# A decode-step kernel on one core: the last 128-row tile of the output weights goes to 32 partitions in four small loads

## The chip, the cores and the metric

The kernel runs on one core of a Trainium2 chip. The metric is the device time of one execution in microseconds (us). Five engines work side by side: PE (TensorE, matrix products; it loads its stationary operand with a weight load, "PEld", ahead of each matmul), DVE (VectorE), ACT (ScalarE), POOL (GpSimd) and SP (SyncE, which here only issues transfers). They wait for each other on semaphores. Transfers between DRAM and the on-chip memory are carried by 16 DMA engines.

## The reference: what is computed

One token for each of 4 sequences, model width 512. From `x` (4 x 512) a layer norm gives `xn`, and the result is `x + s * g`, where

- `s` is an attention over the last W = 1024 rows of a cache: 32 query heads share 8 key/value heads of width 128, so that each key/value head `g` serves 4 query heads. `q = xn @ wq`, then softmax of `q k^T / sqrt(128)`, times `v`, and last the projection `o @ wo` with `wo` of 4096 x 512;
- `g = silu(gelu(layernorm(xn) @ w1 + b1) @ w2 + b2)`, with `w1` 512 x 1792 and `w2` 1792 x 512.

Everything is bf16 in DRAM. About 29 MB are read: 8 MB each for the used parts of the keys and values, 4 MB for `wq`, 3.5 MB for `w1` and `w2`, and 4 MB for `wo`.

## The kernel before, in words

The order of the work is written out by hand. `_Program` keeps one list of operations for each engine (`pe`, `dve`, `act`, `gp`, `sp`); an operation names the operations it depends on, and `emit` puts a semaphore wait ahead of it. Each engine runs its list in order, so the order of the lists is the schedule. A DMA has a semaphore of its own, which must reach 16.

**Transfers.** SP issues nearly all of them in one queue, in this order: half of `wq`, keys of heads 0 and 1, the other half of `wq`, keys 2 to 7, values 0, `w1`, values 1, `w2`, values 2 to 7, and then `wo` in six loads (lines 470 to 476), called here load 0 to load 5. Loads 0, 1 and 2 bring two heads each (1 MB, 4 KB in a row of the DMA), load 3 brings head 6 (512 KB), load 4 brings three quarters of head 7 (rows with `i` = 0 to 2, 384 KB, 3 KB in a row), and load 5 the last quarter (`i` = 3, 128 KB, 1 KB in a row). ACT issues the small ones: `x`, `b1`, `b2` and, at line 251, `x` once more as 16 rows of 128 (`x16`, two loads of 8 rows).

**Attention.** For each head, PE transposes the keys (`T`, line 278), DVE copies them out of PSUM (line 284), PE forms the scores (`S`, lines 293 and 297), ACT takes the exponential (line 305). Then for each head `PV` (line 315) multiplies by the values, a matmul by ones (line 321) forms the denominators, and `epilogue` on DVE (lines 328 to 333) divides and writes `OTb`.

**MLP.** `mlp1` to `mlp4` are put between the `PV`s of the first heads. `mlp1` multiplies by `w1` in rows: 16 matmuls of 512 columns and four for the bias (lines 400 to 408); it is the last reader of `w1_sb`. The result `g_sb` is ready at 58 us.

**Output projection.** `to_rows` (line 478) spreads the normalized outputs of all heads over the partitions: 16 small matmuls with a selection matrix `sel` that POOL builds at the start (line 231), and one DVE copy to `OW` (line 493). Then `wo(k, rows)` (line 499) runs for loads 0 to 5 in order: for each 128-row tile (head `g`, quarter `i`) four matmuls of 128 columns (line 507), 128 matmuls in all, all adding into one place in PSUM (`psM`). Each `wo(k)` waits for its load. So load 0 has 32 matmuls, loads 1 and 2 have 32 each, load 3 has 16, load 4 has 12 and load 5 has 4.

**Tail.** DVE multiplies by `g` (line 534), PE transposes (line 538), DVE adds `x16` (line 540), SP writes the 4 KB out (line 542) and waits for it.

Of the kernel before, what the change touches and what calls it, by code (L numbers as in the profile page):

```python
# [16 lines left out]
class _Program:  # L17
# [10 lines left out]
    def add(self, eng, fn, *deps):  # L28
        op = _Op(eng, fn, deps)
        self.ops[eng].append(op)  # L30
        return op
# [42 lines left out]
def bass_recurrent_scan__sliding_block_cached__mixer_channel_mlp__decode_kernel(  # L74
# [20 lines left out]
    B, D = 4, 512  # L95
# [26 lines left out]
    wo_sb = sb([128, HKV, 4, D], BF16)  # L122
    w1_sb = sb([128, 4, F], BF16)
    w2_sb = sb([128, FC, D], BF16)
    kt_buf = sb([128, NKT, UT * 128], BF16)
    P_buf = sb([128, HKV, NC * 16], BF16)

# [30 lines left out]
    b1_sb = sb([1, F], BF16)  # L158
    b2_sb = sb([4, 128], BF16)
    sel = sb([128, 4, 32], BF16)  # L160
    OW = sb([128, 4, HKV * 4], BF16)
    hT = sb([128, 64], BF16)

    OTb = sb([128, HKV * 16], BF16)
# [39 lines left out]
    def load_v(g):  # L204
        d_v[g] = pg.dma("sp", "v%d" % g, lambda e: e.dma_start(  # L205
            kv_buf[:, (HKV + g) % NS, :, :].rearrange("p c d -> p (c d)"), cache_rows(A_v_cache, g)),
            t_last[(HKV + g) % NS] if HKV + g >= NS else None)
# [11 lines left out]
    for g in range(2, HKV):  # L219
# [11 lines left out]
    c_sel = add("gp", lambda e: e.affine_select(  # L231
        sel[:, :, :], ones_bf[:, :], [[1, 4], [4, 32]], ALU.is_equal, 0.0,
        base=0, channel_multiplier=-1), c_1)
    c_xT = add("gp", lambda e: e.memset(xT[:, :, :], 0.0))
    c_yT = add("gp", lambda e: e.memset(yT[:, :, :], 0.0))
    c_z = add("gp", lambda e: e.memset(zero_bf[:, :], 0.0))
# [11 lines left out]
    v = add("dve", lambda e: e.bn_aggr(mv1[:, :], st1[:, :]), v)  # L248
    v = add("dve", lambda e: e.tensor_single_scalar(vt1[:, :], mv1[:, 1:2], EPS, ALU.add), v)
    a = add("act", lambda e: e.activation(sq1[:, :], vt1[:, :], AF.Sqrt), v)  # L250
    d_x16 = [pg.dma("act", "x16%d" % i, lambda e, i=i: e.dma_start(
        x16[8 * i:8 * i + 8, :], x_r[8 * i:8 * i + 8, :])) for i in range(2)]
    v = add("dve", lambda e: e.reciprocal(rstd1[:, :], sq1[:, :]), a)
    v = add("dve", lambda e: e.tensor_scalar(xn32[:, :], x32[:, :], mv1[:, 0:1], rstd1[:, 0:1],
                                             op0=ALU.subtract, op1=ALU.mult), v)
# [53 lines left out]
    def PV(g):  # L309
        pso = psO[g % 2]  # L310

        def fn(pe):
            last = None
            for c in range(NC):
                last = pe.matmul(pso[:, 0:16], kv_buf[:, (HKV + g) % NS, c, :],  # L315
                                 P_buf[:, g, c * 16:(c + 1) * 16],
                                 start=(c == 0), stop=(c == NC - 1))
            return last
        pv_op[g] = add("pe", fn, ex[g], d_v[g], ep[g - 2] if g >= 2 else None)

        den[g] = add("pe", lambda pe: pe.matmul(psS[g % 2][:, 0:512], ones_bf[:, :], P_buf[:, g, :],  # L321
                                                start=True, stop=True),
                     ex[HKV - 2 + g % 2], ep[g - 2] if g >= 2 else None)

    def epilogue(g):
        pso = psO[g % 2]
        cs = slice(g * 16, (g + 1) * 16)
        v = add("dve", lambda e: e.tensor_reduce(  # L328
            den_sb[:, cs], bass.AP(psS[g % 2], 0, [[512, 128], [1, 16], [16, NC]]),
            AX.X, ALU.add), den[g])  # L330
        v = add("dve", lambda e: e.reciprocal(rden[:, cs], den_sb[:, cs]), v)  # L331

        ep[g] = add("dve", lambda e: e.tensor_tensor(  # L333
            bass.AP(OTb, g * 16, [[HKV * 16, 128], [1, 4], [4, 4]]),
            pso[:, 0:16], rden[:, cs], ALU.mult), v, pv_op[g])
# [59 lines left out]
    def mlp1():  # L395
        def fn(pe):
            last = None
            for c in range(4):
                for s in range(4):
                    pe.matmul(psK[0][32 * s:32 * s + 32, 0:1024].bitcast(F32), yT[:, c, :],  # L400
                              bass.AP(w1_sb, c * F + K0[s], [[4 * F, 128], [1, 4], [FC, 128]]),
                              start=(c == 0), stop=False, tile_position=(0, 32 * s))
            for s in range(4):
                last = pe.matmul(psK[0][32 * s:32 * s + 32, 0:1024].bitcast(F32),
                                 ones_bf[0:1, 0:32],
                                 bass.AP(b1_sb, K0[s], [[F, 1], [1, 4], [FC, 128]]),
                                 start=False, stop=True, tile_position=(0, 32 * s))
            return last
        t = add("pe", fn, v_xyT, d_w1, d_b1, *[cp[n] for n in range(NUN - NB, NUN)])
        a = add("act", lambda e: e.activation(f32k(0), h_ps, AF.Square), t)  # L410
        v = add("dve", lambda e: e.scalar_tensor_tensor(f32k(1), f32k(0), 1.0 / GELU_K, h_ps,  # L411
                                                        op0=ALU.add, op1=ALU.mult), a)
        mlp["t"] = add("act", lambda e: e.activation(f32k(2), f32k(1), AF.Tanh,
                                                     scale=GELU_C * GELU_K), v)

    def mlp2():
        v = add("dve", lambda e: e.tensor_scalar(f32k(3), f32k(2), 0.5, 0.5,
                                                 op0=ALU.mult, op1=ALU.add), mlp["t"])
        v = add("dve", lambda e: e.tensor_tensor(hb, f32k(3), h_ps, ALU.mult), v)  # L419

        def fn(pe):
            last = None
            for t in range(4):
                last = pe.transpose(psK[2][:, t * 128:(t + 1) * 128],  # L424
                                    kt_buf[:, 4, t * 128:(t + 1) * 128], ident[:, :])
            return last
        t = add("pe", fn, v, cp[NUN - 1], cp[NUN - 2])

        mlp["h"] = add("dve", lambda e: e.tensor_copy(
            bass.AP(hT, 0, [[64, 128], [4, 16], [1, 4]]),  # L430
            bass.AP(psK[2], 0, [[1024, 128], [32, 16], [1, 4]])), t)

    def mlp3():
        def fn(pe):
            last = pe.matmul(psM[:, PS_Z:PS_Z + 16], b2_sb[:, :],
                             bass.AP(ident, 0, [[128, 4], [1, 4], [0, 4]]),
                             start=True, stop=False, skip_group_check=True)
            for k in range(FC):
                s = min(k // 4, 2) if k < FC - 4 else 3
                n = (k - K0[s]) * 16 + s * 4  # L440
                for c in range(4):
                    last = pe.matmul(psM[:, PS_Z + c * 4:PS_Z + (c + 1) * 4],
                                     w2_sb[:, k, c * 128:(c + 1) * 128], hT[:, n:n + 4],
                                     start=False, stop=(k == FC - 1), skip_group_check=True)
            return last
        t = add("pe", fn, mlp["h"], d_w2, d_b2, c_id)
        mlp["tz"] = add("act", lambda e: e.activation(
            tz_sb[:, :], psM[:, PS_Z:PS_Z + 16], AF.Tanh, scale=0.5), t)
# [17 lines left out]
        w2_sb[:, :, :], B_w2.rearrange("(p c) o -> p c o", c=FC)))  # L466
    for g in range(2, HKV):
        load_v(g)

    wo_r = A_wo.rearrange("(g p i) o -> p g i o", g=HKV, i=4)  # L470
    d_wo = []
    for n, (g0, g1, i0, i1) in enumerate(((0, 2, 0, 4), (2, 4, 0, 4), (4, 6, 0, 4), (6, 7, 0, 4),
                                          (7, 8, 0, 3), (7, 8, 3, 4))):
        d_wo.append((g0, g1, i0, i1, pg.dma("sp", "wo%d" % n, lambda e, g0=g0, g1=g1, i0=i0, i1=i1:
                                            e.dma_start(wo_sb[:, g0:g1, i0:i1, :],  # L475
                                                        wo_r[:, g0:g1, i0:i1, :]))))

    def to_rows(g0, g1):

        psx = psS[0]  # L480

        def fn(pe):
            last = None
            for i in range(4):
                for j in range(4):
                    last = pe.matmul(psx[32 * j:32 * j + 32, i * 32 + g0 * 4:i * 32 + g1 * 4],
                                     sel[:, i, :],
                                     bass.AP(OTb, g0 * 16 + j * 4,
                                             [[HKV * 16, 128], [16, g1 - g0], [1, 4]]),
                                     start=True, stop=True)  # L490
            return last
        t = add("pe", fn, ep[g1 - 1], c_sel, ex[HKV - 2])
        return add("dve", lambda e: e.tensor_copy(
            OW[:, :, g0 * 4:g1 * 4],
            psx[:, 0:128].rearrange("p (i n) -> p i n", i=4)[:, :, g0 * 4:g1 * 4]), t)

# [16 lines left out]
            return last  # L513
        return add("pe", fn, d, rows, mlp["g"])

    for g in range(HKV):
        PV(g)
        if g == 0:
            epilogue(0)
            mlp1()  # L520
        if g >= 2:
            epilogue(g - 1)
        if g == 1:
            mlp2()
            mlp3()
        if g == 2:
            mlp4()
    epilogue(HKV - 1)
    rows = to_rows(0, HKV)
    for k in range(len(d_wo)):  # L530
        t_w = wo(k, rows)


    v = add("dve", lambda e: e.tensor_tensor(  # L534
# [61 lines left out]
```

## Time and profile before

| what | value |
|---|---|
| time, median of 3 runs | 77.09 us (77.07 to 77.11) |
| profiled execution, its own time | 77.07 us |
| span of that execution in the profile | 75.3 us (1.8 us lie around it) |
| busy: PE, PEld, DVE, ACT, POOL | 50.0, 39.8, 39.3, 9.8, 4.6 us |
| DMA | 28.99 MB, mean 385 GB/s |
| 42 to 67 us | DMA share 1.00 to 1.01, 420 GB/s; granted PE clock 0.82, then 0.50 |
| 70.0 to 72.5 us | DMA share 0.40, PE busy 2.30 us, granted clock 0.50 |
| 72.5 to 75.3 us | the tail: 0.38 us of PE, 0.46 us of DVE |

The profile shows one execution. Times inside it are counted from the start of the span. The granted clock is the share of its full speed at which PE was allowed to run. Matmuls are pipelined: a matmul that is shown with 166 ns can start 27 ns after the one ahead of it. "issue" as the cause of an idle time means that the engine waited for nothing that the profile shows. A DMA that is spread over all 16 DMA engines counts its semaphore up 16 times, once as each engine's share lands, and the trace has the time of each of the sixteen. The trace also has every packet that a DMA engine moved (start, duration, size, queue), though not the engine's number.

### The profile page before, as it was taken

The numbers are of one execution on the slowest core, as the hardware profiler recorded it, in microseconds if no ns is written. First come the engines' busy times: TensorE is split into PE (matmuls) and PEld (weight loads), VectorE is DVE, ScalarE is ACT, GpSimd is POOL, SyncE is SP. The second block draws the span as 40 slices with busy tenths as digits, with TensorE's granted clock in tenths as the row PEclk, the third lists the DMA queues.
The fourth block names the chain that finished last, engine by engine and source line by source line (L and its number), as shares of the span: only waits on it lengthen the run. The fifth ranks groups of instructions, "written<-read, shape, count | busy, mean of one in ns | idle before, by whom it ended". The sixth has DMA issues, their size and how long they took to land.

```text
span 75.3 us, 2297 instructions
## 1 busy us (share of the span) xinstructions
PE 50.0 (66%) x1046; PEld 39.8 (53%) x1058; DVE 39.3 (52%) x82; ACT 9.8 (13%) x16; POOL 4.6 (6%) x14
## 2 busy tenths in 40 slices
PE   0000039993859949987997994999069879818770
PEld 0000039992359939976997860104049576518740
DVE  0778107786058967985996424001664679770010
ACT  0611000000090303111130630003300000000000
POOL 6980000000000000000000000000000000000000
PEclk9999999999999999999999999569755555555555
DMA  1899999998999999999999999999999999999600
GB/s 36 244 455 405 420 422 479 435 444 370 427 422 431 422 418 431 427 414 466 401 420 453 406 443 390 427 431 409 427 427 440 418 401 416 418 420 416 252 25 2
DMA packets 4219, 28.99 MB, mean 385 GB/s; under 512 B 493, under 2 KB 625, under 8 KB 1650
## 3 DMA queue, kind: packets, MB, share of 16 engines
q1 hardware_dynamic: 4160, 28.84, 92.2%
q8 instruction: 8, 0.13, 0.6%
q10 hardware_dynamic: 50, 0.01, 0.1%
q14 instruction: 1, 0.01, 0.0%
HBM read 28.85 MB, written 0.00 MB: 383 GB/s over the span
## 4 chain that ended last, share of the span: by engine, by line
DMA 36%; PE 35%; SPq 16%; issue 5%; DVE 4%
DMA wo_sb<-in_A_wo_dram 24%; PE psK L278 22%; SPq L475 15%; DMA kv_buf<-in_A_k_cache_dram 12%; PE psS L297 7%; PE psO L362 3%; DVE kt_buf L284 2%; DVE q_sb L368 1%; PE psK L374 1%; PE psM L507 1%; PE psK L346 1%; PE psS L538 1%; SPq L212 1%; SPq L205 0%; DVE o_bf L540 0%
## 5 line engine op out<-in xcount | busy, mean ns | idle before, releaser
L278 PE MATMUL psK<-ident,kv_buf 128*128 128x128 bf16 x256 | 21.2, 237 | 11.8 <-DMA kv_buf<-in_A_k_cache_dram 10.6
L284 DVE COPY kt_buf<-psK 128x1024 bf16<-128x1024 bf16 x32 | 21.3, 691 | 8.7 <-PE psK L278 8.6
L278 PEld LDWEIGHTS psK<-ident,kv_buf 128*128 128x128 bf16 x256 | 17.1, 108 | 11.1 <-DMA kv_buf<-in_A_k_cache_dram 10.6
L297 PE MATMUL psS<-qT,kt_buf 128*128 128x16 bf16 x256 | 10.4, 169 | 1.7 <-issue 1.1
L297 PEld LDWEIGHTS psS<-qT,kt_buf 128*128 128x128 bf16 x256 | 9.4, 96 | 3.0 <-issue 2.1
L315 PEld LDWEIGHTS psO<-P_buf,kv_buf 128*128 128x128 bf16 x256 | 7.4, 102 | 3.0 <-issue 3.0
L315 PE MATMUL psO<-P_buf,kv_buf 128*128 128x16 bf16 x256 | 8.0, 173 | 1.0 <-DVE OTb L333 0.6
L328 DVE TENSOR_REDUCE den_sb<-psS 128x16 f32<-128x512 f32 x8 | 5.5, 691 | 4.2 <-PE psO L315 4.0
L305 ACT ACTIVATE P_buf<-psS 128x512 bf16<-128x512 f32 x8 | 4.8, 597 | 17.1 <-PE psS L297 17.1
L400 PE MATMUL psK<-w_sb,yT 128*32 128x512 bf16 x16 | 4.9, 1093 | 1.3 <-issue 1.3
L507 PE MATMUL psM<-OW,wo_sb 128*128 128x4 bf16 x128 | 3.9, 166 | 1.1 <-issue 0.6
L507 PEld LDWEIGHTS psM<-OW,wo_sb 128*128 128x128 bf16 x128 | 3.6, 104 | 1.4 <-issue 1.2
L411 DVE SCALAR_TENSOR_TENSOR kt_buf<-kt_buf,psK 128x512 f32<-128x512 f32 x1 | 0.7, 686 | 6.4 <-ACT kt_buf L410 6.4
L534 DVE TENSOR_TENSOR sg_sb<-psM,g_sb 128x16 f32<-128x16 f32 x1 | 0.2, 185 | 4.7 <-PE psM L507 4.7
L400 PEld LDWEIGHTS psK<-w_sb,yT 128*32 128x32 bf16 x16 | 0.5, 114 | 3.8 <-issue 3.8
L369 ACT ACTIVATE q_sb<-psO 128x512 bf16<-128x512 f32 x1 | 0.6, 597 | 13.5 <-PE psO L362 13.5
L424 PE MATMUL psK<-ident,kt_buf 128*128 128x128 bf16 x4 | 0.6, 307 | 2.4 <-DVE kt_buf L419 2.4
L331 DVE RECIPROCAL rden<-den_sb 128x16 f32<-128x16 f32 x8 | 2.0, 253 | 0.3
L362 PE MATMUL psO<-wq_sb,xT 128*32 128x512 bf16 x32 | 1.9, 380 | 0.3 <-DVE xT L351 0.3
L246 DVE CAST P_buf<-x_bf 4x512 f32<-4x512 bf16 x1 | 0.8, 795 | 2.4 <-DMA x_bf<-in_A_x_dram 2.4
L237 POOL TENSOR_SCALAR_AFFINE_SELECT negm<-zero_bf 128x512 bf16<-128x512 bf16 x1 | 1.9, 1852 | 0.1
L321 PE MATMUL psS<-P_buf,ones_bf 128*128 128x512 bf16 x3 | 1.8, 587 | 0.0
(64 smaller groups left out, 27.4 us busy)
## 6 DMA issues: line engine op xcount, KB each, us to landing
kv_buf<-in_A_k_cache_dram SPq DMA_DIRECT2D x8, 1024.0 KB, 19.9
kv_buf<-in_A_v_cache_dram SPq DMA_DIRECT2D x8, 1024.0 KB, 22.8
wq_sb<-in_A_wq_dram SPq DMA_DIRECT2D x2, 2048.0 KB, 11.3
w_sb<-in_B_w_dram SPq DMA_DIRECT2D x2, 1792.0 KB, 27.9
wo_sb<-in_A_wo_dram SPq DMA_DIRECT2D x3, 1024.0 KB, 24.3
wo_sb<-in_A_wo_dram SPq DMA_DIRECT2D x1, 512.0 KB, 21.5
wo_sb<-in_A_wo_dram SPq DMA_DIRECT2D x1, 384.0 KB, 18.2
wo_sb<-in_A_wo_dram SPq DMA_DIRECT2D x1, 128.0 KB, 18.0
```

The costliest lines, as they stand in the source:

```text
L237: c_neg = add("gp", lambda e: e.affine_select(negm[:, :], zero_bf[:, :], [[0, 32], [1, 4], [0, 4]], ALU.is_equal, NEG, base=0, channel_mul ...
L278: last = pe.transpose(psK[n % NB][:, j * 128:(j + 1) * 128], kv_buf[:, g, u * UT + j, :], ident[:, :])
L284: cp[n] = add("dve", lambda e: e.tensor_copy(kt_buf[:, n % NKT, :], psK[n % NB][:, 0:1024]), t, sc.get(n - NKT))
L297: last = pe.matmul(psS[g % 2][:, c * 16:(c + 1) * 16], kt_buf[:, n % NKT, j * 128:(j + 1) * 128], qT[:, g * 16:(g + 1) * 16], start=False, ...
L305: ex[g] = add("act", lambda e: e.activation(P_buf[:, g, :], psS[g % 2][:, 0:512], AF.Exp, scale=SCALE), sc[n])
L315: last = pe.matmul(pso[:, 0:16], kv_buf[:, (HKV + g) % NS, c, :], P_buf[:, g, c * 16:(c + 1) * 16], start=(c == 0), stop=(c == NC - 1))
L328: v = add("dve", lambda e: e.tensor_reduce(den_sb[:, cs], bass.AP(psS[g % 2], 0, [[512, 128], [1, 16], [16, NC]]), AX.X, ALU.add), den[g])
L331: v = add("dve", lambda e: e.reciprocal(rden[:, cs], den_sb[:, cs]), v)
L362: last = pe.matmul(psO[m // 4][32 * s:32 * s + 32, 0:512], xT[:, c, :], wq_sb[:, c, m * 512:(m + 1) * 512], start=(c == 0), stop=(c == 3), ...
L400: pe.matmul(psK[0][32 * s:32 * s + 32, 0:1024].bitcast(F32), yT[:, c, :], bass.AP(w1_sb, c * F + K0[s], [[4 * F, 128], [1, 4], [FC, 128]]) ...
L475: e.dma_start(wo_sb[:, g0:g1, i0:i1, :], wo_r[:, g0:g1, i0:i1, :]))))
L507: last = pe.matmul(psM[:, PS_W + c * 4:PS_W + (c + 1) * 4], wo_sb[:, g, i, c * 128:(c + 1) * 128], OW[:, i, g * 4:(g + 1) * 4], start=firs ...
```

## The change

Load 5, the 128-row tile of head 7 with `i` = 3, is no longer one load to 128 partitions. It becomes four loads of 32 rows of 1 KB each to partitions 0 to 31 of `wox_sb`, which lies in the memory of `w1_sb` (so they wait for the matmuls of `mlp1`). The DRAM side of each has an outermost dimension of 4 and an inner one of 8. They stand in SP's queue after load 3 and ahead of the rest of head 7, which now comes as a new load 4 (`i` = 0 and 1, 256 KB) and a new load 5 (`i` = 2, 128 KB). The bytes are the same. On PE, four matmuls of 128 rows are replaced by sixteen of 32 rows (`wo_x`), run after load 3's, and one matmul more in `to_rows` forms their other operand, which DVE copies to `OWx` in a copy of its own ahead of the copy to `OW`. POOL makes one more small constant (`selx`). Besides, `x16` comes in three loads of 7, 6 and 3 rows.

```diff
+    wox_sb = w1_sb[0:32, :, :].rearrange("p c f -> p (c f)")[:, 0:4 * D].rearrange(
+        "p (j o) -> p j o", j=4)
+    c_selx = add("gp", lambda e: e.tensor_copy(
+        selx[:, :], bass.AP(sel, 96, [[128, 128], [1, 4], [4, 8]])), c_sel)
...
-    d_x16 = [pg.dma("act", "x16%d" % i, lambda e, i=i: e.dma_start(
-        x16[8 * i:8 * i + 8, :], x_r[8 * i:8 * i + 8, :])) for i in range(2)]
+    d_x16 = [pg.dma("act", "x16%d" % i, lambda e, i=i, n=n: e.dma_start(
+        x16[i:n, :], x_r[i:n, :])) for i, n in ((0, 7), (7, 13), (13, 16))]
...
-    for n, (g0, g1, i0, i1) in enumerate(((0, 2, 0, 4), (2, 4, 0, 4), (4, 6, 0, 4), (6, 7, 0, 4),
-                                          (7, 8, 0, 3), (7, 8, 3, 4))):
...
+    for n, g0 in enumerate((0, 2, 4)):
+        load_wo(n, g0, g0 + 2, 0, 4)
+    load_wo(3, 6, 7, 0, 4)
+
+    for j in range(4):
+        d_wox.append(pg.dma("sp", "wox%d" % j, lambda e, j=j: e.dma_start(
+            wox_sb[:, j, :],
+            bass.AP(A_wo.tensor, (7 * 512 + 128 * j + 3) * D, [[4 * D, 4], [16 * D, 8], [1, D]])), mlp["w1"]))
+    load_wo(4, 7, 8, 0, 2)
+    load_wo(5, 7, 8, 2, 3)
...
     def to_rows(g0, g1):
...
+            last = pe.matmul(psx[0:32, 128:144], selx[:, :],
+                             OTb[:, 7 * 16:8 * 16], start=True, stop=True)
             return last
+        t = add("pe", fn, ep[g1 - 1], c_sel, c_selx, ex[HKV - 2])
+        rows_x = add("dve", lambda e: e.tensor_copy(OWx[:, :], psx[0:32, 128:144]), t)
...
+    def wo_x():
+        def fn(pe):
+            last = None
+            for j in range(4):
+                for c in range(4):
+                    last = pe.matmul(psM[:, PS_W + c * 4:PS_W + (c + 1) * 4],
+                                     wox_sb[:, j, c * 128:(c + 1) * 128],
+                                     OWx[:, j * 4:(j + 1) * 4],
+                                     start=False, stop=False, skip_group_check=True)
+            return last
+        return add("pe", fn, rows_x, *d_wox)
...
+    rows_x, rows = to_rows(0, HKV)
     for k in range(len(d_wo)):
         t_w = wo(k, rows)
+        if k == 3:
+            wo_x()
```

More of the change, by code (lines that the diff above doesn't have):

```diff
@@ L160, in bass_recurrent_scan__sliding_block_cached__mixer_channel_mlp__decode_kernel @@
     sel = sb([128, 4, 32], BF16)
+    selx = sb([128, 32], BF16)
     OW = sb([128, 4, HKV * 4], BF16)
+    OWx = sb([32, 16], BF16)
     hT = sb([128, 64], BF16)
@@ L408, in fn @@
             return last
-        t = add("pe", fn, v_xyT, d_w1, d_b1, *[cp[n] for n in range(NUN - NB, NUN)])
+        t = mlp["w1"] = add("pe", fn, v_xyT, d_w1, d_b1, *[cp[n] for n in range(NUN - NB, NUN)])
         a = add("act", lambda e: e.activation(f32k(0), h_ps, AF.Square), t)
@@ L468, in bass_recurrent_scan__sliding_block_cached__mixer_channel_mlp__decode_kernel, with load_wo @@
         load_v(g)
+    for g in range(HKV):
+        PV(g)
+        if g == 0:
+            epilogue(0)
+            mlp1()
+        if g >= 2:
+            epilogue(g - 1)
+        if g == 1:
+            mlp2()
+            mlp3()
+        if g == 2:
+            mlp4()
+    epilogue(HKV - 1)
     wo_r = A_wo.rearrange("(g p i) o -> p g i o", g=HKV, i=4)
     d_wo = []
-    for n, (g0, g1, i0, i1) in enumerate(((0, 2, 0, 4), (2, 4, 0, 4), (4, 6, 0, 4), (6, 7, 0, 4),
-                                          (7, 8, 0, 3), (7, 8, 3, 4))):
-        d_wo.append((g0, g1, i0, i1, pg.dma("sp", "wo%d" % n, lambda e, g0=g0, g1=g1, i0=i0, i1=i1:
-                                            e.dma_start(wo_sb[:, g0:g1, i0:i1, :],
-                                                        wo_r[:, g0:g1, i0:i1, :]))))
+    d_wox = []
+    def load_wo(n, g0, g1, i0, i1):
+        d_wo.append((g0, g1, i0, i1, pg.dma("sp", "wo%d" % n, lambda e: e.dma_start(
+            wo_sb[:, g0:g1, i0:i1, :], wo_r[:, g0:g1, i0:i1, :]))))
+    for n, g0 in enumerate((0, 2, 4)):
[7 more added lines that the diff above has]
+    load_wo(5, 7, 8, 2, 3)
     def to_rows(g0, g1):
@@ L490, in fn @@
                                      start=True, stop=True)
-            return last
-        t = add("pe", fn, ep[g1 - 1], c_sel, ex[HKV - 2])
-        return add("dve", lambda e: e.tensor_copy(
+            last = pe.matmul(psx[0:32, 128:144], selx[:, :],
+                             OTb[:, 7 * 16:8 * 16], start=True, stop=True)
+            return last
+        t = add("pe", fn, ep[g1 - 1], c_sel, c_selx, ex[HKV - 2])
+        rows_x = add("dve", lambda e: e.tensor_copy(OWx[:, :], psx[0:32, 128:144]), t)
+        return rows_x, add("dve", lambda e: e.tensor_copy(
             OW[:, :, g0 * 4:g1 * 4],
@@ L514, in wo @@
         return add("pe", fn, d, rows, mlp["g"])
[L516 to L529, printed above, removed]
+    def wo_x():
[10 more added lines that the diff above has]
+    rows_x, rows = to_rows(0, HKV)
     for k in range(len(d_wo)):
         t_w = wo(k, rows)
+        if k == 3:
+            wo_x()
     v = add("dve", lambda e: e.tensor_tensor(
```

## The prediction, made before the changed kernel ran

> **What bounds the kernel now.** I read three views in this order: the chain that ended last, PE's timeline over the last microseconds, and the DMA section of the page together with the sixteen landings of each load. The chain first (start, us, what):
>
> ```profile
> 53.69 18.16 DMA wo_sb<-in_A_wo_dram
> 71.86 0.05 issue
> 71.90 0.60 PE psM L507 x16
> 72.50 0.02 issue
> 72.52 0.20 DVE sg_sb L534
> ```
>
> The end hangs on load 4 of `wo`, which lands at 71.86, then on 16 matmuls (12 of load 4, 4 of load 5), then on the tail of 2.8 us, which the change doesn't touch. A reader could stop here and call the kernel bound by loads. PE's timeline says more:
>
> ```profile
> 67.19 0.30 PE L486 MATMUL psS<-OTb,sel 128*32 128x32 bf16 x16 [1.30 <-DVE OTb L333]
> 68.00 1.55 PE L507 MATMUL psM<-OW,wo_sb 128*128 128x4 bf16 x53 [0.51 <-DVE OW L493]
> 70.13 2.35 PE L507 MATMUL psM<-OW,wo_sb 128*128 128x4 bf16 x75 [0.58 <-issue]
> ```
>
> 53 matmuls take 1.55 us, one is shown with 0.166, so they start (1.55 - 0.166) / 52 = 26.7 ns apart (granted clock 0.50). Then PE stands for 0.58 us in the middle of load 1, which had landed at 67.06: it waits for no data. The DMA section names the other traffic:
>
> ```profile
> q8 instruction: 8, 0.13, 0.6%
> q14 instruction: 1, 0.01, 0.0%
> ```
>
> These are PE's instructions, in packets of 16 KB. The packet records have one at 67.84, and PE resumes 2.29 us after it; earlier ones at 25.51, 32.21 and 38.29 are followed by the chain's "issue" pieces, which end at 27.95, 34.43 and 40.45, 2.2 to 2.4 us later. So the stop is PE waiting for its program. From 70.13 on, 74 x 0.0267 + 0.166 = 2.14 us of the 2.35 are matmuls, and only 0.21 is the wait for load 4. **Loads and PE are nearly tied at the end**: what the loads gain beyond 0.21 us, PE does not pass on, and PE's own added work counts.
>
> The landings (us) of the last loads show why loads are late:
>
> ```
> load 3: 69.15 69.16 69.19 69.20 69.30 69.39 69.43 69.49 | 70.11 70.57 70.72 70.72 70.74 70.77 70.82 70.93
> load 4: 70.08 70.14 70.14 70.18 70.28 70.34 70.39 70.42 | 71.05 71.49 71.62 71.63 71.68 71.71 71.72 71.86
> load 5: 70.42 70.47 70.48 70.51 70.62 70.64 70.73 70.73 | 71.37 71.82 71.96 71.96 72.01 72.05 72.05 72.17
> ```
>
> Eight DMA engines are early, seven are some 1.4 us late, one 0.7 us; I take each to have carried one of the seven q8 packets up to 67.84 (0.88 to 0.96 us long), or the 8 KB q14 packet at 41.24 (0.31 us). Engines that work without a pause start a packet when the last one ends, to within 4 ns, so the packets can be strung into sixteen chains. The loads of 4 rows at the start (`x_bf`, `b2`) and of 1 row (`b1`) each land 4 times and once, and their packets lie in four of the chains; I take these to be the engines that a load spread over four uses. Three of the four are early (last data of load 5 at 70.15, 70.20, 70.29), **the fourth is the one with the q14 packet** (71.06, landing 71.37).
>
> **The loads, step by step.** 1 KB packets of load 5 start 42.4 ns apart, 3 KB packets of load 4 117.6 ns; 2 KB lies on the line between, 80 ns (estimate). Each engine has 8 rows of a full load.
> - The twelve other engines: 8 x 117.6 + 8 x 42.4 ns become 8 x 80 + 8 x 42.4, 0.30 us less. Their last landing goes from 72.17 to 71.87.
> - The four: 32 rows of 1 KB more, 32 x 42.4 = 1.36 us, four semaphore writes of 6 ns and one more `x16` row (20 ns) on some, less 0.30: +1.08 us. The three early ones land at 70.47 to 70.62 + 1.08 = 71.55 to 71.70. The late one lands at 71.37 + 1.08 = **72.45**, after the 72.17 of before.
> - The four loads land on the late engine at about 71.5 (its load 4 began at 69.77; + 1.38 + 0.31 from data to landing).
> - If such a load were spread over 16 engines instead, the bytes of each engine stay, and the last landing is 72.17 and four semaphore writes.
>
> The Trainium skill, "DMA: Bandwidth & Descriptors", section "Why a DMA increments its semaphore by 16 and not by 1", says the number of engines is the largest divisor up to 16 of the outermost dimensions of both sides, and that they are the lowest-numbered: with 4 and 32 here, four.
>
> **PE, step by step.** The program up to `to_rows` is unchanged on PE, so I let the stop end at 70.13 again. The added matmul of `to_rows` takes one pair of instructions, so 52 instead of 53 matmuls are ahead of the stop. After it come 128 - 4 + 16 - 52 = 88. PE reaches `wo_x` at 70.13 + 60 x 0.0267 = 71.73, when its loads are in, new load 4 at 72.16 (landed by 71.6 on the twelve, 72.11 on the late one) and new load 5 at 72.37. Alone it would end at 70.13 + 87 x 0.0267 + 0.166 = 72.62 against 72.48: +0.13 us. Two terms are not in the trace:
> - A pair with 32 rows: between 7 ns (line 486, 32 columns: (0.30 - 0.19) / 15) and 26.7 ns (line 507, the same 128 columns). I take 26.7; the other end saves 16 x 19.7 ns = 0.31 us.
> - The four semaphores that `wo_x` waits for are two more wait instructions of 51 ns. One ahead of line 538 (72.21) ran while matmuls kept their spacing: between 0 and 0.10 us, I take 0.
>
> The skill's "TensorE: Matmul & The Clock Gate", section "LDWEIGHTS (loading the stationary operand)", puts the price on columns and not on rows, like my choice. Against my stop speaks "Runtime: NRT & Kernel Launch", "Instruction fetch mechanics": crossing a block is "mostly hidden". The row has 0.58 us unhidden; with none PE would reach load 5 by about 71.8, and the loads alone would decide.
>
> **Sum.** New load 5 lands last at 72.45 on the late engine. Before, load 4's landing at 71.86 gave starts at 71.90, 71.95, 71.97, 72.00; so the last of four starts 0.14 after the landing and ends 0.17 later: 72.76 against 72.48, +0.28 us. This hides both unknown PE terms (72.37 + 0.10 is still ahead of 72.49). On the profiled execution: 77.07 + 0.28 = **77.35 us**; the median shown, 77.09, is 0.02 above it.
>
> **Costed at nothing.** DVE's added copy to `OWx` (0.17 to 0.29 us by lines 351 and 493) stands ahead of the copy to `OW`; `wo(0)` and all PE work up to the stop move by it, and the stop of 0.58 us swallows it; without that cover it costs 0.2 us. The added `to_rows` matmul likewise. POOL's `selx` (0.2 to 0.5 us beside its neighbours) delays `xT`, whose first reader is at 18.34, while POOL is through at 5.5. ACT's third `x16` issue (0.28 to 0.44 us) ends near 5.5; its next work starts at 6.79, on DVE. SP's four added issues (0.4 to 0.6 us each, up to 5.4 when the queue is full, as for load 5) come behind load 3's at 53.65; the queue then holds some 80 rows for each engine, so load 5 is issued by about 64, before 69 when it is needed. `mlp1`, which the four wait for, is through by 51.6. DVE's third wait for `x16` passes while PE transposes.
>
> **Rivals.**
> - *PE alone is the bound*: the q14 packet falls on none of the four engines. Then the last landing is 71.87 and PE ends 0.13 us later, 77.20 us, up to 77.30 with the waits. For it: the trace doesn't say what assigns that packet. Against: the three runs agree to 0.04 us, as they would if packets always fell alike.
> - *The loads' gain shows* (the other side, faster): place, the stop at 69.55. If PE's instructions come so early that the stop is under about 0.1 us, PE reaches load 5 by 71.87, and if no late engine is among the four, the end is 71.87 + 0.31 = 72.18: -0.30, 76.77 us. Cheap 32-row pairs alone, without a late engine, give -0.18, 76.89. It decides from 0.3 us less PE time on. Against: nothing ahead of the stop changes on PE.
> - *A 16 KB packet falls on one of the four*: that engine lands 1.08 after the latest now, about 73.2, and `wo_x` waits too: +1.0, 78.1 us. Against: none of seven did.
> - *The four loads use 16 engines*: last landing 72.2, reached by PE at 72.37: +0.13 or less, 77.1 to 77.2.
>
> **Chances.** Late engine among the four, 77.35 (77.25 to 77.45): 0.46. PE alone: 0.22, split between the bound of "same" on either side (0.08 same, 0.14 slower; a difference of 0.2%, 0.15 us, is about what can be told from none). Gain shows: 0.18. Packet on one of the four: 0.06. Sixteen engines: 0.08, same. Faster 0.18, same 0.16, slower 0.66. The range runs from the gain to well above the forecast, 76.75 to 77.6, and leaves out the 78.1.
>
> **What would show it.** Right: the landings of each `wox` load count four and not sixteen; the last landing of new load 5 stands alone near 72.45, the others end near 71.87; 52 or 53 matmuls of line 542 ahead of a stop of about 0.4 to 0.6 us ending at 70.1; no wait between load 3's matmuls and `wo_x`. Wrong: the stop missing or ending elsewhere; the last landing on an engine that got nothing more; sixteen matmuls of `wo_x` in much less than 0.43 us.

## The result and the profile after

| | median | all runs | profiled execution, its span |
|---|---|---|---|
| before | 77.09 us | 77.07 to 77.11 (4) | 77.07, 75.3 us |
| after | 77.69 us | 77.62 to 77.91 (4) | 77.91, 76.2 us |

The ratio is 1.0083 [1.0062, 1.0103]: slower by 0.60 us. The forecast was 77.35 in a range of 76.75 to 77.6, so the sign is right and the size is outside the range. The profiled execution of after is the slowest of its four, so its tail shows some 0.2 us more than the median.

The chain that ended last, of the kernel after (start, us, what):

```profile
49.56 22.05 DMA wo_sb<-in_A_wo_dram
71.61 0.05 issue
71.65 0.59 PE psM L542 x16
72.24 0.13 issue
72.37 0.56 PE psM L556 x16
72.94 0.49 PE psM L542 x12
73.43 0.02 issue
73.45 0.20 DVE sg_sb L570
```

Before, the last load named here was load 4, issued at 53.69, and DVE's `sg_sb` began at 72.52. Now it is load 3, issued at 49.56, a load that the change did not touch. It lands last at 71.61 (before: 70.93), and PE's work follows it nearly without a pause. The later loads are close behind, though: the sixteen matmuls of `wo_x` start at 72.37, 0.13 us after the last small load lands (72.24), and the last four matmuls start at 73.15, 0.05 us after the last landing of load 5 (73.10), and end at 73.41. That is 0.31 us after the landing, as in the forecast's sum. So load 3, the small loads and load 5 are nearly tied, and the chain view names the first of them. PE's timeline of after:

```profile
65.85 0.30 PE L518 MATMUL psS<-OTb,sel 128*32 128x32 bf16 x16 [1.30 <-DVE OTb L340]
66.73 1.53 PE L542 MATMUL psM<-OW,wo_sb 128*128 128x4 bf16 x52 [0.58 <-DVE OW L528]
68.85 0.46 PE L542 MATMUL psM<-OW,wo_sb 128*128 128x4 bf16 x12 [0.59 <-issue]
70.02 1.02 PE L542 MATMUL psM<-OW,wo_sb 128*128 128x4 bf16 x32 [0.70 <-DMA wo_sb<-in_A_wo_dram]
71.65 0.59 PE L542 MATMUL psM<-OW,wo_sb 128*128 128x4 bf16 x16 [0.62 <-DMA wo_sb<-in_A_wo_dram]
72.37 0.56 PE L556 MATMUL psM<-OWx,w_sb 32*128 32x4 bf16 x16
72.87 0.55 PE L542 MATMUL psM<-OW,wo_sb 128*128 128x4 bf16 x12
```

52 matmuls, then the stop of 0.59 us, as forecast, but 1.28 us earlier (it ends at 68.85 and not at 70.13). PE has time to spare now: it waits 0.70 us for load 2 and 0.62 us for load 3. The bracket of the fifth line is what to look at: a wait for load 3 was in no step of the forecast. The amount of instruction traffic is that of before:

```profile
q8 instruction: 8, 0.13, 0.6%
q14 instruction: 1, 0.01, 0.0%
```

Its place in time is not. PE's eighth 16 KB packet, at 71.74 before, comes at 69.98 here and lasts 1.13 us, beside the last loads. That alone does not make loads late: in runs 2 and 3 below it comes at 70.39 and 70.24, and load 5 lands by 72.27 and 72.17, within 0.1 us of before; and the slowest run, to partitions 64-79 and 96-111, has it at 71.78.

The landings of after (us):

```
load 3: 69.22 ... 69.75 (eight) | ... 71.61            before: 69.15 ... 69.49 | ... 70.93
wox 0:  69.77 69.89 70.04 | 71.16       wox 1: 70.26 70.39 70.52 | 71.57
wox 2:  70.75 70.83 70.90 | 71.91       wox 3: 71.06 71.20 71.35 | 72.24
load 5: 70.63 70.71 70.94 70.94 71.04 | 71.90 ... 72.49 72.69 | 73.10
```

Each `wox` load lands four times, three engines early and one late, and the last landing of load 5 stands alone. That is the forecast's picture; but the forecast had it at 72.45, with 71.87 for the latest of the others. From one small load to the next the late engine takes 0.33 to 0.41 us and the early ones at most 0.50, which leaves no room for a packet of 1.13 us: the rival that put a 16 KB packet on one of the four, at 78.1 us, is not what happened.

**Where the time came from.** The activity of each microsecond, kernel before and then kernel after (window, length, busy time and instructions of PE, PEld, DVE, ACT, POOL, then PE clock, DMA share, GB/s):

```profile
69.00:70.00 1.00, 0.55 (x21) 0.49 (x19) 0.00 (x0) 0.00 (x0) 0.00 (x0) 0.50 0.97 386
70.00:71.00 1.00, 0.87 (x33) 0.87 (x33) 0.00 (x0) 0.00 (x0) 0.00 (x0) 0.50 0.65 252
71.00:72.00 1.00, 0.94 (x35) 0.86 (x33) 0.00 (x0) 0.00 (x0) 0.00 (x0) 0.50 0.35 124
```

```profile
69.00:70.00 1.00, 0.31 (x12) 0.23 (x9) 0.00 (x0) 0.00 (x0) 0.00 (x0) 0.50 1.14 413
70.00:71.00 1.00, 0.98 (x32) 0.93 (x32) 0.00 (x0) 0.00 (x0) 0.00 (x0) 0.50 0.73 222
71.00:72.00 1.00, 0.38 (x15) 0.35 (x14) 0.00 (x0) 0.00 (x0) 0.00 (x0) 0.50 0.59 200
```

Read the last two columns together. From 70 to 71, before has its engines busy 0.65 of the time and moves 252 GB/s, 388 for a full share. After is busier, 0.73, and moves less, 222 GB/s: 304 for a full share. The engines are not idle and not given more bytes; their packets last longer. The packet records give the sizes: outside this stretch a 4 KB packet takes 159 ns, 3 KB 121, 2 KB 84 and 1 KB 46, nearly always to the nanosecond. In after, from about 69.9 to 70.6, most 4 KB packets take 200 to 271 ns, and many of 1 KB 50 to 80. I add up what the packets of loads to 73.6 us took over these four figures, from 69.0 on, and call it **lost packet time** (in us of a DMA engine, summed over all 16): 3.76 us in after, 0.21 in before.

### The profile page after: what moved, and what is told of

The parts are those of the page before. It is cut to its first block, busy times and chain, and to the rows that moved or that the text cites. A ratio compares the mean times of both kernels' runs of the same rounds, so it can differ in the third digit from the quotient of the medians.

```text
span 76.2 us, 2333 instructions
## 1 busy us (share of the span) xinstructions
PE 49.9 (66%) x1059; PEld 39.4 (52%) x1071; DVE 39.6 (52%) x83; ACT 9.8 (13%) x16; POOL 4.8 (6%) x15
## 4 chain that ended last, share of the span: by engine, by line
DMA 41%; PE 33%; SPq 12%; DVE 5%; issue 4%
DMA wo_sb<-in_A_wo_dram 29%; PE psK L285 20%; DMA kv_buf<-in_A_k_cache_dram 12%; SPq L496 11%; PE psS L304 7%; DVE kt_buf L291 4%; PE psO L369 3%; PE psM L542 1%; DVE q_sb L375 1%; PE psK L381 1%; PE psM L556 1%; PE psK L353 1%; SPq L217 1%; PE psS L574 1%; SPq L210 0%
## 5 line engine op out<-in xcount | busy, mean ns | idle before, releaser
L285 PE MATMUL psK<-ident,kv_buf 128*128 128x128 bf16 x256 | 20.4, 230 | 12.1 <-DMA kv_buf<-in_A_k_cache_dram 10.8
L285 PEld LDWEIGHTS psK<-ident,kv_buf 128*128 128x128 bf16 x256 | 16.1, 103 | 11.8 <-DMA kv_buf<-in_A_k_cache_dram 10.8
```

The costliest lines, as they stand in the source:

```text
L285: last = pe.transpose(psK[n % NB][:, j * 128:(j + 1) * 128], kv_buf[:, g, u * UT + j, :], ident[:, :])
```

## Experiments

Twelve runs. Times are medians; "before" ran again beside each group of runs on the same chip (77.03 to 77.07). The ratio is taken from all runs and has a 95% interval; it can differ a little from the quotient of the medians. Lost packet time and the last landing of load 5 are those of the one profiled execution, which can lie some tenths of a us from the median. All edits are against the kernel after, unless it says otherwise.

| run | time, us | ratio to before | lost packet time, us | last landing |
|---|---|---|---|---|
| before | 77.09 | | 0.21 | 72.17 |
| after | 77.69 | 1.0083 [1.0062, 1.0103] | 3.76 | 73.10 |
| sixteen engines | 77.86 | 1.0115 [1.0090, 1.0141] | 2.65 | 72.58 |
| before, load 5 as 4 x 32 | 77.06 | 1.0009 [0.9997, 1.0020] | 0.00 | 72.27 |
| PE's part alone | 77.22 | 1.0025 [1.0005, 1.0044] | 0.00 | 72.17 |
| four loads early | 78.45 | 1.0202 [1.0159, 1.0246] | 6.34 (60.8 to 63.6) | 72.87 |
| own partitions | 77.70 | 1.0085 [1.0070, 1.0100] | 3.33 | 72.80 |
| own partitions, sixteen | 77.31 | 1.0030 [1.0014, 1.0047] | 0.20 | 72.61 |
| one load, four engines | 77.56 | 1.0063 [1.0045, 1.0080] | 2.65 | 72.76 |
| one load, partitions 0-31 | 77.57 | 1.0071 [1.0045, 1.0098] | 1.64 | 72.70 |
| to 0-15 and 32-47 | 77.43 | 1.0050 [1.0033, 1.0067] | 0.21 | 72.44 |
| to 64-79 and 96-111 | 78.93 | 1.0242 [1.0218, 1.0267] | 11.85 | 73.89 |
| to 16-31 and 48-63 | 78.19 | 1.0149 [1.0124, 1.0174] | 11.35 | 73.39 |
| eight engines, 0-63 | 77.32 | 1.0037 [1.0023, 1.0050] | 0.00 | 72.71 |

**1. Sixteen engines.** Is it the confinement to four engines?

```diff
-            bass.AP(A_wo.tensor, (7 * 512 + 128 * j + 3) * D, [[4 * D, 4], [16 * D, 8], [1, D]])), mlp["w1"]))
+            bass.AP(A_wo.tensor, (7 * 512 + 128 * j + 3) * D, [[4 * D, 32], [1, D]])), mlp["w1"]))
```

(`selx` takes its columns in the plain order.)

> The changed kernel with one edit: the DRAM side of each of the four 32-row loads has an outermost dimension of 32 instead of 4, so that each spreads over 16 DMA engines; PE's work, SP's queue and the bytes are the same. Late-engine theory (the four engines get 24 rows more, one of them is late anyway): no engine gets more, the last landing goes back to about 72.2, PE's added matmuls cost 0.13 us, time about 77.2 us. Traffic theory (rows of 1 KB beside the last full loads slow the packets of all engines, 1.2 to 1.6 times between 69.8 and 70.6 us in the changed kernel): the slow stretch stays, 77.5 us or more. PE theory (the sixteen matmuls and their four waits are the cost): as the changed kernel, 77.6 to 77.7.

77.86 us. The loads land sixteen times each, no engine carries more bytes than before, and it is no faster. The packets are stretched here too (69.3 to 70.4). The confinement to four engines by itself is not what made the forecast too small.

**2. Load 5 of the kernel before, written 4 x 32.** It was to put one load of 128 partitions on four engines.

```diff
+        if n == 5:
+            d_wo.append((g0, g1, i0, i1, pg.dma("sp", "wo%d" % n, lambda e: e.dma_start(
+                wo_sb[:, 7, 3, :],
+                bass.AP(A_wo.tensor, (7 * 512 + 3) * D, [[128 * D, 4], [4 * D, 32], [1, D]])))))
+            continue
```

> The kernel before with one edit: load 5's DRAM side is written as 4 x 32 rows, so that one load to 128 partitions is carried by four DMA engines, 32 rows each; PE's work is that of before. Late-engine theory: the late one of the four has 24 rows of 42.4 ns more, its landing goes from 71.37 to about 72.4, the end moves by 0.2: about 77.3 us; the other engines land load 5 no later than load 4, by 71.9. Traffic theory: a stretch of slow packets, all engines' load 4 late, 77.5 us or more. PE theory: 77.1, as before.

It landed sixteen times: 32 steps of 4 rows are one step of 128, so the two dimensions became one of 128, and the transfers are those of the kernel before. So it says nothing on four engines and serves as a second profile of before: no lost packet time. It also shows that the place of PE's stop varies without the change: PE runs before's program, and here the stop ends at 69.22 and not at 70.13.

**3. PE's part alone.** PE, DVE, POOL and `x16` as after, the loads as before; PE reads `wox` from memory that was not loaded, so the last quarter of head 7 is left out.

```diff
-    for j in range(4):
-        d_wox.append(...
...
-    load_wo(4, 7, 8, 0, 2)
-    load_wo(5, 7, 8, 2, 3)
+    load_wo(4, 7, 8, 0, 3)
+    load_wo(5, 7, 8, 3, 4)
...
```

> The changed kernel's PE, DVE and POOL work with the loads of before (128 partitions, 384 KB and 128 KB); the sixteen 32-row matmuls read what lies in the memory of w1, so the last quarter of head 7 is left out of the result. Late-engine theory and traffic theory: landings as before (72.17), PE reaches its last four matmuls at about 72.4, +0.13: 77.2 us. PE theory: 77.6 to 77.7.

77.22 us, +0.19 with an interval from +0.04 to +0.34; the forecast's term was +0.13. PE's timeline of this run:

```profile
69.09 0.46 PE L541 MATMUL psM<-OW,wo_sb 128*128 128x4 bf16 x12 [0.59 <-issue]
69.72 1.01 PE L541 MATMUL psM<-OW,wo_sb 128*128 128x4 bf16 x32 [0.18 <-DMA wo_sb<-in_A_wo_dram]
70.96 0.59 PE L541 MATMUL psM<-OW,wo_sb 128*128 128x4 bf16 x16 [0.22 <-DMA wo_sb<-in_A_wo_dram]
71.48 0.58 PE L555 MATMUL psM<-OWx,w_sb 32*128 32x4 bf16 x16
```

Here PE is early as in after, but waits only 0.22 us for load 3, which lands at its old time. No packet is stretched. So the stretch belongs to the four loads, not to the program of PE. (This profile is of an execution of 77.01 us, no slower than before; where the 0.19 us of the median come from is not shown.)

**4. The four loads early.** They stand ahead of load 0, into the memory of `wq_sb`. If their cost is only one of the end, it is hidden there.

```diff
+    for j in range(4):
+        d_wox.append(pg.dma("sp", "wox%d" % j, lambda e, j=j: e.dma_start(
...
     for n, g0 in enumerate((0, 2, 4)):
         load_wo(n, g0, g0 + 2, 0, 4)
```

> The changed kernel with the four small loads issued ahead of load 0 instead of behind load 3 (their memory is then that of wq, which is free by then); same bytes on each engine, same PE work. Late-engine theory: the late one of the four is as late at the end, last landing about 72.4 to 72.5, 77.3 to 77.4 us. Traffic theory: the slow stretch moves to about 60 us, where other work hides it, and the tail's packets run at full speed: 77.3 to 77.4; if the time stays at 77.6 to 77.7 with slow packets in the tail, the four loads' place beside the last loads is not their cause.

78.45 us, the worst yet. The stretch went with the loads: it is gone from the end and stands at 61.1 to 63.4, about where they land (62.40 to 63.55). It cost 6.34 us of engine time; before has 0.55 in the same stretch. The page's GB/s line of this run (40 slices of 1.9 us):

```profile
GB/s 28 258 413 419 423 430 494 430 413 383 430 430 425 421 426 430 426 408 444 451 394 429 447 405 413 434 413 421 430 430 426 415 318 406 421 421 400 205 1 2
```

The 33rd slice, 61.0 to 62.9 us, has 318 between 415 and 406: nearly a quarter of 1.9 us lost, some 0.4 us in a kernel whose loads never pause, and the last landing is 0.70 us later than before. So there is no cover for it at this place either, and other memory on the same partitions does not remove it. (The four runs lie apart, 77.96 to 78.79, and the profile is of the fastest of them, so the size is rough.)

**5 to 8. Which side of the transfer?** After the first four, two theories stood: A, the loads all write to partitions 0 to 31; B, each reads from a region of 128 KB, or there are four loads for one. Four kernels, all with the tile's loads in the same place in the queue. Own partitions: load `j` to partitions 32`j` to 32`j`+31 of the tile's own memory, multiplied by four matmuls of 128 rows as before.

```diff
-            wox_sb[:, j, :],
+            wo_sb[32 * j:32 * j + 32, 7, 3, :],
```

> The changed kernel, but the four loads go to the tile's own partitions in the whole buffer (load j to partitions 32j to 32j+31), so that together they cover all 128, and the tile is multiplied by four matmuls of 128 rows as before. Each load still reads the same rows on the same four engines. Theory A (all engines are slowed because the four loads all write to partitions 0 to 31): no stretched packets near 70 us, a 4096 B packet stays near 160 ns and a 1 KB one near 45 ns; the last landing is that of the late one of the four engines, near 72.4, and the time 77.2 to 77.4. Theory B (each load reads a region of 128 KB at a time, or four loads in place of one disturb the engines by their number): the stretch stays, 4096 B packets of 200 to 270 ns between 69.5 and 70.6, last landing 72.8 to 73.1, time 77.6 to 77.8.

The same over sixteen engines (source dimensions 32 and D):

> The run with own partitions, with each of the four loads over sixteen engines (rows in order, two for each engine, no reordering of the tile). Theory A: no stretch, last landing near the 72.2 of the kernel before, time 77.0 to 77.15. Theory B: stretch as in the changed kernel over sixteen engines, time 77.6 to 77.9.

One load to 128 partitions on four engines, by an order of rows that does not merge:

```diff
+        wo_sb[:, 7, 3, :],
+        bass.AP(A_wo.tensor, (7 * 512 + 3) * D, [[4 * D, 4], [16 * D, 32], [1, D]])), mlp["w1"]))
```

> One load of the tile to all 128 partitions on four engines (source order 4 x 32 with a stride that can't be merged), in the place of the four loads; four matmuls of 128 rows. The rows of the tile come in another order than their multipliers, so the last quarter of head 7 is mis-paired. Its semaphore shows four landings if the load is on four engines. Theories A and B both: no stretch, because one load writes all partitions and reads the whole 512 KB region; what is left is the forecast's own term, the late one of the four engines, with a last landing near 72.4 and 77.2 to 77.4. If the stretch shows here too, both fall, and confining a load to four engines is back as the cause.

One load to partitions 0 to 31, four rows for each, over sixteen engines:

```diff
+        wox_sb[:, :, :],
+        bass.AP(A_wo.tensor, (7 * 512 + 3) * D, [[4 * D, 32], [128 * D, 4], [1, D]])), mlp["w1"]))
```

> The changed kernel with one load in place of the four: 128 rows of 1 KB to partitions 0 to 31, four rows for each, over sixteen engines. Theory A (partitions 0 to 31): the stretch stays, 4096 B packets of about 200 ns, time 77.6 to 77.9. Theory B (regions of 128 KB, or the number of loads): no stretch, last landing near 72.2, and the time that of the run with PE's part alone, 77.15 to 77.3.

Neither theory lives. Theory B wants no stretch with one load; both runs with one load have it (2.65 and 1.64 us lost). Theory A wants none where the loads cover all partitions; own partitions on four engines has it in full (3.33 us, 77.70), and one load to all 128 partitions on four engines too (2.65). But the destination does matter: own partitions over sixteen engines and run 1 differ in nothing on the DMAs but their destination, and one has 0.20 us lost, the other 2.65. And the number of engines matters: own partitions on four and on sixteen differ in that and in the order of rows. What four engines to all partitions, and sixteen engines to few partitions, may have in common is that **an engine writes partitions that in a whole load another engine writes**. That is theory C of the next three runs. (One run already speaks against its plain form; see "What stays open".)

Own partitions on four engines shows a second thing. Its PE has none of the sixteen matmuls of 32 rows, and its time is that of after:

```profile
71.56 0.59 PE L543 MATMUL psM<-OW,wo_sb 128*128 128x4 bf16 x16 [0.71 <-DMA wo_sb<-in_A_wo_dram]
72.11 0.25 PE L557 MATMUL psM<-OW,wo_sb 128*128 128x4 bf16 x4
72.57 0.55 PE L543 MATMUL psM<-OW,wo_sb 128*128 128x4 bf16 x12 [0.21 <-DMA wo_sb<-in_A_wo_dram]
```

PE waits 0.71 us for load 3 and 0.21 for load 4 (which lands at 72.52): with stretched loads, PE's added work is not what costs.

**9 to 11. Same rows, same four engines, other partitions.** Only the destination is changed, two rows to each of 16 partitions:

```diff
-            wox_sb[:, j, :],
+            wox_sb[0 + 32 * (j % 2):16 + 32 * (j % 2), j - j % 2:j - j % 2 + 2, :],
```

(64 or 16 more on the partitions in the other two.)

> The changed kernel with the same four loads of the same rows on the same four engines, and only their destination changed: two rows of 1 KB to each of 16 partitions, 0 to 15 or 32 to 47, so that the four engines write four partitions each. TensorE's instructions are unchanged, so the last quarter of head 7 is multiplied with other rows than the reference's. Theory C (the partitions that an engine writes in a whole load of 128 partitions are its own; writing others, while their engine is still at work, slows both): the Trainium skill, DMA: Bandwidth & Descriptors, section The descriptor swizzle, gives engines 0 to 3 the partitions 0 to 15 and 32 to 47 in such a load. If that holds here, no stretch, 4096 B packets near 160 ns, last landing near the forecast's 72.4, time 77.25 to 77.5. Theory D (few engines with a run of 1 KB rows slow the others wherever they write): stretch as in the changed kernel, 77.6 to 77.9. Theory E (crowding on few partitions): stretch stronger than in the changed kernel, since each load now has half its partitions, 77.7 to 78.1.

> As the run to partitions 0 to 15 and 32 to 47, with the destination 64 partitions further (64 to 79 and 96 to 111); TensorE still reads partitions 0 to 31 of the memory of w1, so the last quarter of head 7 is left out. Theory C: these are the partitions of four other engines, so the stretch is back, 4096 B packets over 200 ns and 77.6 to 77.9. Theories D and E: as their value for the run before.

> As the run to partitions 0 to 15 and 32 to 47, with the destination 16 partitions further (16 to 31 and 48 to 63); the last quarter of head 7 is multiplied with other rows or old values. Theory C: partitions of four other engines again, stretch and 77.6 to 77.9, unless those engines are among the early ones and have ended, then less. Theories D and E: as their value for the first of the three runs.

77.43, 78.93 and 78.19 us. The activity of two microseconds, first of the run to partitions 0-15 and 32-47, then of the run to 64-79 and 96-111:

```profile
70.00:71.00 1.00, 0.61 (x23) 0.61 (x23) 0.00 (x0) 0.00 (x0) 0.00 (x0) 0.50 0.73 278
71.00:72.00 1.00, 1.00 (x43) 1.00 (x39) 0.00 (x0) 0.00 (x0) 0.00 (x0) 0.50 0.39 129
```

```profile
70.00:71.00 1.00, 0.58 (x22) 0.58 (x22) 0.00 (x0) 0.00 (x0) 0.00 (x0) 0.50 0.78 156
71.00:72.00 1.00, 0.73 (x28) 0.65 (x25) 0.00 (x0) 0.00 (x0) 0.00 (x0) 0.50 0.78 209
```

The same sources on the same number of engines: 278 GB/s at a share of 0.73 (381 for a full share, as in before) against 156 at 0.78 (200). In the second run nearly all 4 KB packets take 300 to 324 ns, twice their time, for a full microsecond, and most of 1 KB 72 to 106. In the first, all but one of 438 packets take their usual time. Crowding on few partitions (theory E) is out: both runs use 32. Few engines with runs of short rows (theory D) is out: both use four. Theory C has the direction right in all three, though the two stretched runs cost more than the 77.6 to 77.9 us that it foretold. The partitions of the undisturbed run are those that the Trainium skill ("DMA: Bandwidth & Descriptors", section "The descriptor swizzle") gives to the four lowest engines in a transfer to 128 partitions. The same page, in its section "Back-pressure in remote DMA", says of transfers between cores that a saturated destination port clogs the path back to the engines that share it. Something like it would fit engines that are slowed without being among the four, but these loads come from DRAM, and no run here shows ports.

The landings of the undisturbed run are the forecast's. Load 5 lands last at 72.44, alone (forecast 72.45), and the latest of the twelve others at 71.84 (71.87). What ends it last is PE, and not that landing: the last matmul ends at 73.05, while the landing and the forecast's 0.31 us make 72.75.

```profile
68.27 1.53 PE L542 MATMUL psM<-OW,wo_sb 128*128 128x4 bf16 x52 [0.58 <-DVE OW L528]
70.39 1.74 PE L542 MATMUL psM<-OW,wo_sb 128*128 128x4 bf16 x60 [0.59 <-issue]
72.06 0.58 PE L556 MATMUL psM<-OWx,w_sb 32*128 32x4 bf16 x16
72.57 0.48 PE L542 MATMUL psM<-OW,wo_sb 128*128 128x4 bf16 x12
```

In this run the stop ends at 70.39, 0.26 us later than forecast, and from there no load holds PE up. The steps between matmuls at `wo_x` and at load 4 add 0.17 us. With both, PE's forecast end of 72.62 becomes 73.05.

**12. Eight engines, their own partitions.** A version that might have been faster: 32 rows of each load on eight engines, to partitions 0 to 31 and 32 to 63, two rows to a partition, so PE has eight matmuls of 64 rows in place of four of 128.

```diff
+            wox_sb[32 * (j // 2):32 * (j // 2) + 32, j % 2, :],
+            bass.AP(A_wo.tensor, (7 * 512 + 128 * j + 3) * D, [[4 * D, 8], [32 * D, 4], [1, D]])), mlp["w1"]))
```

> The changed kernel with the four loads on eight engines instead of four, and to the partitions that these eight write in a whole load (0 to 31 for the first two loads, 32 to 63 for the others; two rows of 1 KB to a partition), and with eight matmuls of 64 rows in place of the sixteen of 32. The result is the reference's. Theory C: no stretch, a 4096 B packet near 160 ns; the eight engines get eight 1 KB rows more than in the kernel before less none (+0.34), the other eight get eight fewer (-0.34). If all late engines are among the other eight, the last landing is 71.85 and the time 76.9 to 77.1; if some are among the eight, 72.5 and 77.3 to 77.5. If the stretch is back, theory C is wrong or incomplete, and 77.6 or more.

77.32 us, and not one of 447 packets over its usual time: as theory C foretold, and the time is in its range. Partitions 16 to 31 and 48 to 63 are among those written here, so it is not these partitions by themselves that cost 11.35 us in run 11. It is no faster than before, since three of the eight engines are late ones (the first load lands at 69.36 to 69.72 five times, then 70.47, 70.97, 71.25), and load 5 ends at 72.71. No kernel of these beats the one before.

## Why the prediction was right in sign and wrong in size

The step that failed is the first line of "The loads, step by step": that 1 KB packets stay 42.4 ns apart and longer ones in proportion. Every landing after that was worked out with them. What the runs showed in its place: with the small loads on partitions 0 to 31 the packets last longer for a while (69.9 to 70.6 us: 4 KB 200 to 271 ns and not 159, many of 1 KB 50 to 80 and not 46), and the late engine lands at 73.10 and not at 72.45. The forecast looked at how many rows an engine carries and not at where it puts them.

- *Four engines for each small load*: right, four landings each.
- *The twelve others gain 0.30 us, 71.87*: wrong. They landed by 72.69; with packets undisturbed, 71.84.
- *The late engine at 72.45*: 73.10, alone as forecast; undisturbed, 72.44. Row counts, the spacing of undisturbed packets and the late engine were right, and the term that is missing is the stretch: 0.65 us on this landing, and 0.68 on load 3, which the forecast left where it was.
- *Sum, +0.28*: +0.60 measured. In the profiled execution, the slowest of four, PE's end moved by 0.93 us (72.49 to 73.41): the 0.28 of the sum and the 0.65 of the stretch. The run with the four loads to 0-15 and 32-47, which has the change without the stretch, is at +0.36 (0.25 to 0.52). That this lies near +0.28 is partly luck: its landing is the forecast's, but PE ended it, 0.30 us after the end that the landing would give. The 0.24 between +0.36 and +0.60 is the difference of two medians of different groups, whose intervals overlap a little, so its size is rough; that other partitions cost more is far outside the error (+1.12 and +1.86).
- *PE alone, +0.13*: +0.19 (0.04 to 0.34). A 32-row pair at 26.7 ns: (0.56 - 0.166) / 15 = 26.3 ns, right. The waits of `wo_x`: 0.13 us from landing to start where load 4 had 0.05, so 0.08, within the bounds. In the run to 0-15 and 32-47 the steps at `wo_x` and at load 4 together added 0.17, more than the 0.10 that bounded this term.
- *The stop ends at 70.13 again*: wrong, 68.85, with no effect, since PE then waited for loads. Half of the condition of the rival "the loads' gain shows" came true, PE early; the gain of the loads did not.
- *Sixteen engines, 77.1 to 77.2*: the rival's price was wrong for the same reason, 77.86.
- *Costed at nothing*: nothing of DVE's copy, POOL's constant, `x16` or SP's issues is in the chain's end. Right as far as the chain shows.

**What stays open.** Theory C was put together from runs 1 and 5 to 8 and foretold the next four; it does not give every size, and in its plain form it does not hold. Own partitions over sixteen engines lost only 0.20 us, though by the list of "The descriptor swizzle" nearly every engine there writes partitions of others: each has two partitions of a small load, in order, so that in each load only one of the sixteen is on its own. What sets it apart from run 1 may be how many rows meet on the same partitions at once; no run tests that. Shown is that the destination decides for the same sources and engines, and that engines which keep to the partitions of the list left the other packets undisturbed (two runs); what makes the others collide is open. Own partitions over sixteen engines is also 0.24 us slower than before without a stretch, and its last landing is 72.61; the cause is open. Why PE's stop ends 0.8 to 2.0 us earlier than before in some of these programs (68.12 in eight engines, 68.85 in after, 69.37 in own partitions) and not in others (70.39) is open too; run 2, with PE's program of before, has it at 69.22. And the forecast took each late engine to have carried an instruction packet. The lateness of 1.4 us is longer than such a packet (0.88 to 0.96), and no run tests what makes these engines late.

## What to carry to other kernels

A load that is moved to other engines or other partitions is not priced by its bytes: count the landings, and ask which engines write those partitions in the transfers beside it. Where all DMA engines are busy, a small reshaped load can slow the packets of other loads; here it did so at both places in the queue that were tried. Look at GB/s against the DMA share, and at the durations of packets of one size, before the order of loads. And a load written as 4 x 32 rows landed four times when its two dimensions could not merge, and sixteen times when they could.

## What the runs showed of the hardware

- The kernel with the same 128 rows of 1 KB on the same four engines was slower than before by 0.36 us with partitions 0-15 and 32-47, by 1.12 with 16-31 and 48-63, by 1.86 with 64-79 and 96-111. In the last two, 4 KB packets of other loads went from 159 ns to over 300 meanwhile.
- Undisturbed packets are very regular: 46, 84, 121 and 159 ns for 1, 2, 3 and 4 KB. A longer one is a sign by itself.
- PE stops once in the middle of the last matmuls in each of these programs, with no data to wait for, while the loads fill the engines: 0.58 to 0.96 us in ten of the fourteen profiles, 0.16 to 0.53 in the others.
